# One written order of a fused recurrence and feed-forward kernel exchanged for another

## Chip, cores, metric

One core of a Trainium2 chip. The metric is the device time of one execution in microseconds, taken as the median of several runs; beside it there is one profiled execution, whose trace and page are read here. Its engines are PE (TensorE, with its weight loads shown apart as PEld), DVE (VectorE), ACT (ScalarE), POOL (GpSimd) and SP, which here only issues the transfers.

## What is computed

A gated linear recurrence over 4 sequences of 768 tokens with 8 heads, in chunks, and behind it a feed-forward block on the 3072 tokens of width 256:

```
L = exp(cum[i] - cum[j]) * causal            # cum: running sum of log a
y = (C B^T * L) x + exp(cum) * (C state)     # per chunk and head
state = exp(sum log a) * state + (B * exp(cum_end - cum))^T x
h = y @ w_in                                 # 256 -> 2048
out = softplus(h) @ w_out                    # 2048 -> 256
```

All inputs and the output are float32.

## The kernel before

The 3072 tokens are 24 units of 128 (six to a sequence). A unit needs its decays (on POOL), scores (PE), the product of both (DVE), a state update and the outputs, which are scaled on DVE. The feed-forward part takes the tokens in six blocks j of 512 (four units each) and the hidden width in 16 slices k of 128. Every float32 product of it is made of three matmuls over parts (high x high, high x low, low x high), so the weights, x and the softplus results are split into a high part (an ACT cast) and a low part (a DVE subtraction).

The first 28 projection steps and their surroundings are issued from a text, ORDER. Each word is one step, or one stage of a step that comes again; the digits are its argument:

- la, kb, hc, un, gg, w, gd, cr: transfers issued on SP. w is a piece of the weights (even numbers w_in, odd ones w_out), un a unit's inputs, hc its score operands, gg its growth factors, cr the copies of the split C of a unit into the one buffer c_rows. kb holds constants.
- W: the split of a weight piece, five stages: ACT (two operations), DVE, DVE (the two merges), ACT (high part), DVE (low part, wil or wol). Q: the same for B and C of units from 8 on.
- ft, fr: factors by token and by row (matmuls, then exponentials on ACT; fc is one of their results). D: decays on POOL (the select that writes rm). S: scores. M: scores times decays, in two halves, on DVE (tile m). B, C: scaled B and C (bp, cc). U, T: state and its spread (state, tb). R, I: matmuls of a unit's output. G: the scaling (y on DVE, xh on ACT). X: the low part xl on DVE. gq: growth factors by matmul. zero: c_rows cleared on POOL.
- v, e: for pairs of units from 8 on, the values (update, within) and the ends.
- H: the projection of slice k for the first 256 tokens of block 0. F j.k: the projection (all of it, or its other half where H came before). P j.k: softplus and cast on ACT, low part on DVE. Z j.k: the value step, six matmuls into the two accumulators. K, L: copies of the accumulators of a half block. E: the sums of block 0.
- warmN: N small matmuls on a cleared tile, whose results nothing reads.

Blocks 0 and 1 go through the hidden width in two halves, in the order (0, 0 to 7), (1, 0 to 7), (0, 8 to 15), (1, 8 to 15). Projections, scores, products and updates of the units take their tiles from six PSUM banks, and the two accumulators have one each.

Behind ORDER, from step AHEAD = 28 on, a loop issues one projection and the value step LAG = 4 before it, with the work of units 12 to 23 planned between them. While the flag in_order holds, ACT, DVE and POOL keep the order of the source; from step PINNED on they do not, and the framework's scheduler places their instructions by its own time line. PE and the transfers on SP keep the source's order throughout. In the profile an instruction issued under in_order has line L125 (the helper that pins it), a free one has its own line. A unit from 12 on that is loaded while in_order holds also gets a one-element clearing of its buffer on DVE:

```
if in_order[0] and i >= FIRST:
    V.memset(both[:1, :1, :1], 0)
```

Weight pieces, the operands of later units and one pair of half sums share four buffers (tag wraw); the loads of a piece wait for a free one.

Of the kernel before, what the change touches and what calls it, by code (L numbers as in the profile page):

```python
# [52 lines left out]


ORDER = """
warm8 la w3 w0 hc0 hc1 un2 logr w2 un0 zero loga logr kb un1 growth loga W3 ft0 W3 W0 un3 W3 hc2 S0 W0 ft0 hc3 W0 W3
D0 W0 W3 S1 growth gb gd D1 hc4 M0 W2 un4 gq0 hc5 M0 W0 D2 fr0 gq0 fr2 fr0 ft2 M1 fr2 B1 fr0 B0 I0 W2 fr0 ft2 U0 B2 U1
gq2 U0 B3 C1 U1 G0 S2 gg3 T2 C2 T1 M1 S3 G0 W2 D3 gq2 R1 M2 W2 R2 C3 M2 U2 I1 X0 D4 U2 I2 w1 G1 S4 w4 M3 G1 un6 X1 un5
M3 fr2 hc7 H0 T3 D5 fr2 w6 M4 tl R3 M4 H1 B4 C4 D6 U3 G2 I3 U3 U4 S5 G3 W2 G3 G2 X3 H2 W1 hc6 X2 M5 w5 F0.0 un7 T4 W4
U4 H3 W1 T5 F0.1 C5 B6 W1 R4 P0.0 W4 w7 F0.2 W1 W4 R5 P0.1 W1 F0.3 P0.2 M5 P0.0 U6 I4 W4 U6 D7 I5 P0.1 un9 S6 G5 W6 G4  # L60
gg6 P0.0 S7 W4 P0.3 Z0.0 W6 W5 B7 T7 P0.1 G4 H4 C7 W6 Z0.1 W5 un8 P0.3 M6 P0.2 W5 H5 W6 X4 w8 F0.4 P0.2 R7 P0.3 P0.4
F0.5 W6 Q9 Z0.2 M7 W7 Q9 M7 F0.6 Q9 cr9 M6 G5 D10 gg12 W5 U7 P0.4 I7 U7 D9 Q8 I6 G7 Z0.3 P0.5 X5 G7 P0.6 P0.4 P0.5 W5
F0.7 G6 X7 G6 gg10 Z0.4 X6 Q9 P0.5 w10 F1.0 W7 W7 S9 P1.0 Q8 F1.1 W7 B9 cr8 P0.6 W7 W8 Z0.5 M9 un10 P0.6 P0.7 W8 F1.2
P1.0 P0.7 P1.0 Z0.6 Q8 W8 W10 T8 w9 P0.7 F1.3 Q8 P1.2 W10 P1.2 w12 Z0.7 W8 P1.2 M9 F1.4 L0 W8 D8 P1.1 K0 P1.3 S8 P1.1
F1.5 M8 Q10 P1.1 W12 Z1.0 W10 Q10 w13 P1.4 W12 F1.6 W10 cr10 Q10 W10 W12 Z1.1 W9 M8 un11 C8 D11 W12 F1.7 P1.3 W12 P1.4
Z1.2 P1.7 P1.3 W13 B8 P1.4 F0.8 C9 P1.7 W9 Q11 Q10 Z1.3 P0.8 P1.7 w14 P1.5 v8 P1.5 P1.6 P1.5 W9 F0.9 v8 w15 W13 Z1.4
W13 P0.9 Q11 W9 W13 F0.10 P1.6 P0.8 Z1.5 Q11 P0.8 e8 e8 P0.10 F0.11 W9 P1.6 S10 P0.11 Z1.6 M10 cr11 W14 C10 W13 w11
F0.12 P0.10 B10 W14 P0.9 Q11 Z1.7 W14 S11 K1 F0.13 M11 L1 un13 M10 W11 Z0.8 M11 P0.11 W11 W14 v10 P0.11 W14 P0.13
P0.10 W15 F0.14 v10 C11 P0.13 P0.9 e10 P0.14 F0.15 e10 e10 W11 e10 Z0.9 W15 W11 un12 P0.13 gg8 e10 F1.8 P0.14 W11 W15
Z0.10 W15 P0.12 F1.9 P0.12 P0.15 P0.12 Z0.11 F1.10 P0.15 P0.15 Z0.12 W15 P1.10 P1.10 Z0.13 P1.8 P1.10 e8 P1.9 F1.11  # L70
P0.14 P1.8 e8 Z0.14 e8 P1.11 P1.9 P1.8 P1.9 P1.11 Z0.15 E0 P1.11
"""
HALF = NFT // 2
AHEAD = 28
PINNED = 31
LAG = 4
WRAW = 4
EARLY = 8
# [24 lines left out]
def recurrence_then_ffn(ctx: ExitStack, tc: tile.TileContext, fst, un, alr, w_in, w_out, const, outT):  # L103
# [820 lines left out]
    for s in range(AHEAD, len(steps) + LAG):  # L924
        if s == PINNED:
            in_order[0] = False
# [63 lines left out]
```

## Time and profile before

| | us |
|---|---|
| median of 3 runs | 326.56 |
| lowest, highest | 325.31, 326.64 |
| the profiled execution | 324.59 |
| its span | 322.9 |
| PE busy | 314.8 |
| DVE busy | 201.9 |
| ACT busy | 182.2 |
| POOL busy | 38.6 |

Busy is the time in which an engine executes at least one instruction. Matmuls overlap, so that a busy PE may still start them later than it could; the distance between their starts shows it. The granted clock of PE is in the page and in the answers on stretches of time. A row of the timeline gives the start, the length, the engine, the line, the operation with its tiles, and the number of instructions merged into it; in brackets stands the idle time of the engine before it and what ended it. The 0.98 us before the first matmul and the some 3 us after the last are parts of the span.

### The profile page before, as it was taken

How to read it: one execution, taken by the hardware profiler on the slowest of the kernel's cores; microseconds unless marked ns; L12 is line 12 of the kernel's file. 1: busy time of each engine (PE TensorE's matmuls, PEld its weight loads, DVE VectorE, ACT ScalarE, POOL GpSimd, SP SyncE). 2: the span in 40 equal slices, each digit the busy share in tenths (PEclk: the TensorE clock that was granted, in tenths of full speed). 3: DMA queues.
4: the chain of work that ended last, by engine and by line, in shares of the span. 5: the costliest groups of instructions: out<-in, count | busy, mean ns of one | idle time of the engine just before them, and what ended most of it. 6: DMA issues, size and time to landing. Idle time of an engine off the chain costs nothing.

```text
span 322.9 us, 5266 instructions
## 1 busy us (share of the span) xinstructions
PE 314.8 (98%) x1968; PEld 255.3 (79%) x1968; DVE 201.9 (63%) x354; ACT 182.2 (56%) x333; POOL 38.6 (12%) x42
## 2 busy tenths in 40 slices
PE   7799999999989999999999999999999999999996
PEld 3568878888868888788888788888888888888885
DVE  5999999887793667874646745776653432322222
ACT  5879878895565665555533834745634344544450
POOL 4661030110200001101202101102100000000000
PEclk9999999999999999999999999999999999999999
DMA  7959748553612145344126236135301000100001
GB/s 258 391 175 374 246 130 225 180 167 108 194 52 82 66 149 146 97 143 119 32 100 162 87 110 155 44 106 154 101 0 35 1 2 0 64 1 2 0 0 66
DMA packets 25178, 36.53 MB, mean 113 GB/s; under 512 B 2112, under 2 KB 13504, under 8 KB 25152
## 3 DMA queue, kind: packets, MB, share of 16 engines
q1 hardware_dynamic: 25152, 36.19, 36.4%
q8 instruction: 15, 0.25, 0.3%
q14 instruction: 11, 0.09, 0.1%
HBM read 28.74 MB, written 3.24 MB: 99 GB/s over the span
## 4 chain that ended last, share of the span: by engine, by line
PE 86%; DVE 6%; DMA 4%; ACT 2%; issue 1%; SPq 1%; ACTq 0%; DVEq 0%
PE hp L125 38%; PE acc L125 37%; PE yp L125 6%; PE sp L125 3%; DMA wraw<-in_w_out 3%; DVE w L125 2%; DMA bc<-in_un 1%; PE zp L125 1%; PE end L125 1%; DVE m L125 1%; ACT signs L125 1%; ACT w L125 1%; DVE wol L125 1%; SPq L135 1%; DVE b_rows L288 0%
## 5 line engine op out<-in xcount | busy, mean ns | idle before, releaser
L722 DVE TENSOR_TENSOR gl<-e,gh 128x512 fp32r<-128x512 f32 x65 | 50.9, 787 | 49.0 <-ACT gh L716 48.7
L125 PE MATMUL hp<-xh,wih 128*128 128x512 f32 (+1 forms) x204 | 77.7, 381 | 0.0
L125 PE MATMUL hp<-xh,wil 128*128 128x512 f32 (+1 forms) x204 | 76.9, 377 | 0.6 <-DVE wil L125 0.6
L125 PE MATMUL hp<-xl,wih 128*128 128x512 f32 (+1 forms) x204 | 76.9, 377 | 0.0
L710 ACT ACTIVATE e<-hp 128x512 f32<-128x512 f32 x65 | 38.7, 595 | 64.8 <-PE hp L125 64.2
L125 PE MATMUL acc<-gh,woh 128*128 128x512 f32 x188 | 74.9, 398 | 0.1
L125 PE MATMUL acc<-gl,woh 128*128 128x512 f32 x188 | 73.5, 391 | 0.0
L125 PE MATMUL acc<-gh,wol 128*128 128x512 f32 x188 | 73.2, 390 | 0.0
L125 PEld LDWEIGHTS hp<-xh,wil 128*128 128x128 f32 x204 | 38.3, 188 | 8.2 <-DVE wil L125 1.1
L125 PEld LDWEIGHTS hp<-xh,wih 128*128 128x128 f32 x204 | 38.4, 188 | 7.7 <-DVE y L125 0.8
L125 PEld LDWEIGHTS hp<-xl,wih 128*128 128x128 f32 x204 | 38.4, 188 | 6.8
L716 ACT CAST gh<-e 128x512 fp32r<-128x512 f32 x65 | 40.2, 618 | 5.1 <-PE acc L125 3.5
L125 PEld LDWEIGHTS acc<-gh,woh 128*128 128x128 f32 x188 | 35.4, 188 | 8.5 <-ACT signs L125 0.8
L125 PEld LDWEIGHTS acc<-gh,wol 128*128 128x128 f32 x188 | 35.3, 188 | 7.5
L125 PEld LDWEIGHTS acc<-gl,woh 128*128 128x128 f32 x188 | 35.4, 188 | 6.5 <-DVE gl L722 0.2
L398 POOL TENSOR_SCALAR_AFFINE_SELECT rm<-fc 128x1024 f32<-128x1024 f32 x11 | 16.2, 1477 | 128.2 <-DVE m L453 96.4
L125 DVE TENSOR_TENSOR gl<-e,gh 128x512 fp32r<-128x512 f32 x31 | 21.2, 687 | 10.9 <-ACT gh L125 10.9
L125 POOL TENSOR_SCALAR_AFFINE_SELECT rm<-fc 128x1024 f32<-128x1024 f32 x13 | 18.7, 1443 | 63.7 <-DVE m L125 53.4
L125 ACT ACTIVATE e<-hp 128x512 f32<-128x512 f32 x31 | 18.0, 592 | 12.5 <-PE hp L125 11.0
L125 ACT CAST gh<-e 128x512 fp32r<-128x512 f32 x31 | 18.6, 616 | 5.6 <-PE acc L125 5.4
L125 DVE TENSOR_TENSOR m<-sp,rm 128x512 f32<-128x512 f32 x26 | 17.2, 682 | 1.8 <-PE sp L125 1.2
L453 DVE TENSOR_TENSOR m<-sp,rm 128x512 f32<-128x512 f32 x22 | 14.1, 684 | 3.8 <-PE sp L125 3.8
(104 smaller groups left out, 313.5 us busy)
## 6 DMA issues: line engine op xcount, KB each, us to landing
bc<-in_un SPq DMA_DIRECT2D x16, 512.0 KB
wraw<-in_w_out SPq DMA_DIRECT2D x8, 512.0 KB
wraw<-in_w_in SPq DMA_DIRECT2D x8, 512.0 KB
un<-in_un SPq DMA_DIRECT2D x16, 256.0 KB
out_t<-o SPq DMA_DIRECT2D x9, 256.0 KB
c_rows<-c_all SPq DMA_DIRECT2D x16, 128.0 KB
gg<-gd SPq DMA_DIRECT2D x16, 128.0 KB
c_rows<-kc SPq DMA_DIRECT2D x16, 128.0 KB
```

Of the source, the lines that this page charges most:

```text
L125: return lambda *a, **k: tc.keep_in_program_order(f(*a, **k))
L135: tc.keep_in_program_order(nc.sync.dma_start(out, in_))
L398: Pl.affine_select(out=rm.rearrange("p h c i -> p (h c) i"), in_=fc[:, u].rearrange("p h c -> p (h c)").unsqueeze(2).broadcast_to([P, NH * ...
L453: V.tensor_tensor(mid[i]["m"][:, 4 * g : 4 * g + 4].rearrange("p h t -> p (h t)"), mid[i].pop(("sp", g)), mid[i]["rm"][:, 4 * g : 4 * g + ...
L710: A.activation(e, h, AF.Softplus)
L716: A.copy(gh, e)
L722: V.tensor_tensor(gl, e, gh.bitcast(F32), op=ALU.subtract)
```

## The change

ORDER is replaced by another permutation of the same words, with nine warm-up matmuls in front in place of eight and two single ones between, and PINNED goes from 31 to 37, so that the loop's steps 31 to 36 are issued in source order too.

```
--- before.py
+++ after.py
@@ -53,26 +53,26 @@
 
 
 ORDER = """
-warm8 la w3 w0 hc0 hc1 un2 logr w2 un0 zero loga logr kb un1 growth loga W3 ft0 W3 W0 un3 W3 hc2 S0 W0 ft0 hc3 W0 W3
-D0 W0 W3 S1 growth gb gd D1 hc4 M0 W2 un4 gq0 hc5 M0 W0 D2 fr0 gq0 fr2 fr0 ft2 M1 fr2 B1 fr0 B0 I0 W2 fr0 ft2 U0 B2 U1
-gq2 U0 B3 C1 U1 G0 S2 gg3 T2 C2 T1 M1 S3 G0 W2 D3 gq2 R1 M2 W2 R2 C3 M2 U2 I1 X0 D4 U2 I2 w1 G1 S4 w4 M3 G1 un6 X1 un5
-M3 fr2 hc7 H0 T3 D5 fr2 w6 M4 tl R3 M4 H1 B4 C4 D6 U3 G2 I3 U3 U4 S5 G3 W2 G3 G2 X3 H2 W1 hc6 X2 M5 w5 F0.0 un7 T4 W4
-U4 H3 W1 T5 F0.1 C5 B6 W1 R4 P0.0 W4 w7 F0.2 W1 W4 R5 P0.1 W1 F0.3 P0.2 M5 P0.0 U6 I4 W4 U6 D7 I5 P0.1 un9 S6 G5 W6 G4
-gg6 P0.0 S7 W4 P0.3 Z0.0 W6 W5 B7 T7 P0.1 G4 H4 C7 W6 Z0.1 W5 un8 P0.3 M6 P0.2 W5 H5 W6 X4 w8 F0.4 P0.2 R7 P0.3 P0.4
-F0.5 W6 Q9 Z0.2 M7 W7 Q9 M7 F0.6 Q9 cr9 M6 G5 D10 gg12 W5 U7 P0.4 I7 U7 D9 Q8 I6 G7 Z0.3 P0.5 X5 G7 P0.6 P0.4 P0.5 W5
-F0.7 G6 X7 G6 gg10 Z0.4 X6 Q9 P0.5 w10 F1.0 W7 W7 S9 P1.0 Q8 F1.1 W7 B9 cr8 P0.6 W7 W8 Z0.5 M9 un10 P0.6 P0.7 W8 F1.2
-P1.0 P0.7 P1.0 Z0.6 Q8 W8 W10 T8 w9 P0.7 F1.3 Q8 P1.2 W10 P1.2 w12 Z0.7 W8 P1.2 M9 F1.4 L0 W8 D8 P1.1 K0 P1.3 S8 P1.1
-F1.5 M8 Q10 P1.1 W12 Z1.0 W10 Q10 w13 P1.4 W12 F1.6 W10 cr10 Q10 W10 W12 Z1.1 W9 M8 un11 C8 D11 W12 F1.7 P1.3 W12 P1.4
-Z1.2 P1.7 P1.3 W13 B8 P1.4 F0.8 C9 P1.7 W9 Q11 Q10 Z1.3 P0.8 P1.7 w14 P1.5 v8 P1.5 P1.6 P1.5 W9 F0.9 v8 w15 W13 Z1.4
-W13 P0.9 Q11 W9 W13 F0.10 P1.6 P0.8 Z1.5 Q11 P0.8 e8 e8 P0.10 F0.11 W9 P1.6 S10 P0.11 Z1.6 M10 cr11 W14 C10 W13 w11
-F0.12 P0.10 B10 W14 P0.9 Q11 Z1.7 W14 S11 K1 F0.13 M11 L1 un13 M10 W11 Z0.8 M11 P0.11 W11 W14 v10 P0.11 W14 P0.13
-P0.10 W15 F0.14 v10 C11 P0.13 P0.9 e10 P0.14 F0.15 e10 e10 W11 e10 Z0.9 W15 W11 un12 P0.13 gg8 e10 F1.8 P0.14 W11 W15
-Z0.10 W15 P0.12 F1.9 P0.12 P0.15 P0.12 Z0.11 F1.10 P0.15 P0.15 Z0.12 W15 P1.10 P1.10 Z0.13 P1.8 P1.10 e8 P1.9 F1.11
-P0.14 P1.8 e8 Z0.14 e8 P1.11 P1.9 P1.8 P1.9 P1.11 Z0.15 E0 P1.11
+la warm9 w0 kb hc0 un0 hc2 loga w3 w2 logr loga un1 logr ft0 growth W0 hc1 un2 fr2 ft2 ft0 W0 hc3 W0 D0 S0 fr2 W0 gb
+fr0 W0 S2 D2 growth ft2 M0 gd hc5 fr2 M0 W3 un3 B0 D1 M2 U0 hc4 gq0 fr2 U0 W2 fr0 w4 W3 fr0 B1 gq2 W3 fr0 gq0 U1 W2 S1
+C1 T1 U1 I0 B2 C2 M2 R1 T2 gq2 D3 M1 S3 tl gg3 G0 M1 U2 W3 W2 I1 D4 R2 U2 W2 G1 M3 warm1 G0 I2 G1 X0 S5 C3 T3 G2 X1 S4
+w1 B3 W2 un4 R3 M3 hc6 W4 hc7 warm1 W3 D5 U3 un5 I3 U3 G2 un9 M4 H0 G3 w6 T4 G3 H1 X2 W1 X3 M4 F0.0 W4 D6 H2 P0.0 M5
+C4 F0.1 W4 H3 P0.0 P0.1 W1 F0.2 w5 un6 B4 R4 W1 P0.2 U4 P0.0 W4 I4 U4 W1 S6 M5 un7 P0.2 gg6 W4 D9 P0.1 S7 M6 C5 W1
+F0.3 W6 zero H4 M6 Z0.0 Q9 T5 D7 P0.3 w7 G4 P0.1 R5 F0.4 W6 H5 P0.4 B6 I6 Q9 I5 W6 Q9 U6 Z0.1 G5 C7 w10 Q9 cr9 G5 P0.2
+W6 un8 F0.5 U6 X5 G4 T7 P0.3 Z0.2 M7 P0.4 W6 P0.5 R7 X4 W5 B7 F0.6 M7 P0.4 D8 G6 U7 I7 G6 U7 P0.6 F0.7 G7 W7 P0.3 X6
+W5 Z0.3 G7 P0.6 X7 W7 P0.5 F1.0 W5 Q8 W5 Q8 S9 W5 Q8 F1.1 cr8 M9 W10 W7 w8 Z0.4 P0.6 un11 P0.7 Q8 P0.7 F1.2 W10 W7
+un10 P1.0 P0.7 W7 S8 F1.3 P0.5 W8 W10 B8 Z0.5 w12 P1.2 M8 gg8 P1.1 W8 P1.0 B9 F1.4 W8 Q11 T8 W8 w9 P1.0 Z0.6 W10 M8
+P1.3 M9 D11 P1.3 F1.5 P1.2 P1.3 Q10 D10 Z0.7 C8 P1.5 F1.6 W8 L0 P1.1 Q10 v8 K0 Q10 C9 W12 P1.1 W10 Z1.0 P1.4 Q10 W9
+P1.2 w13 F1.7 cr10 Q11 P1.6 W9 Q11 v8 Z1.1 P1.6 W12 C10 Q11 F0.8 P1.5 w11 P1.5 gg10 Z1.2 W9 W12 w14 P1.6 F0.9 W12 P1.4
+W12 P0.8 B10 Z1.3 P1.4 P1.7 W11 S10 F0.10 P0.9 cr11 W9 P1.7 e8 Z1.4 P1.7 W11 e8 e8 F0.11 W11 gg12 M10 Z1.5 w15 W9 M10
+W14 F0.12 P0.10 W14 S11 P0.10 Z1.6 P0.9 P0.10 W14 F0.13 M11 W14 P0.9 P0.8 P0.11 M11 Z1.7 W11 P0.8 P0.12 v10 K1 C11 L1
+un12 W11 W14 W13 Z0.8 v10 P0.11 e10 e8 F0.14 e10 e10 P0.12 W13 P0.13 Z0.9 P0.12 W15 e10 F0.15 P0.14 e10 P0.14 W13
+Z0.10 P0.14 un13 P0.15 W15 F1.8 W13 P0.11 P0.13 W15 Z0.11 P0.13 P1.8 W15 W13 F1.9 e8 W15 Z0.12 P1.9 P1.8 F1.10 P1.9
+P1.9 Z0.13 P1.8 P0.15 P1.10 P0.15 F1.11 Z0.14 P1.11 P1.11 P1.10 P1.11 Z0.15 E0 P1.10
 """
 HALF = NFT // 2
 AHEAD = 28
-PINNED = 31
+PINNED = 37
 LAG = 4
 WRAW = 4
 EARLY = 8
```

## The prediction

> **What bounds the kernel now.** I read the page's busy lines first, then the stretches, then the matrix unit's waits and the timeline around each of them. Times are us from the span's start; a word of the written order stands for its step (S9, F0.14).
>
> ```profile
> span 322.9 us, 5266 instructions
> PE 314.8 (98%) x1968; PEld 255.3 (79%) x1968; DVE 201.9 (63%) x354; ACT 182.2 (56%) x333; POOL 38.6 (12%) x42
> ```
>
> Next the stretches. The first five lines are of PE alone: stretch, length, PE busy (instructions), granted clock, DMA share, GB/s. The last has all engines: length, PE, weight loads, DVE, ACT, POOL, then clock and DMA.
>
> ```profile
> 0.00:21.20 21.20, 17.19 (x148) 1.00 0.76 267
> 21.20:89.50 68.30, 68.30 (x527) 1.00 0.66 210
> 89.50:92.40 2.90, 2.01 (x10) 1.00 0.03 11
> 109.20:142.00 32.80, 32.67 (x191) 1.00 0.44 136
> 142.00:319.90 177.90, 177.86 (x1024) 1.00 0.22 62
> 20.00:30.00 10.00, 10.00 (x98) 8.11 (x98) 9.72 (x23) 8.11 (x20) 3.42 (x3) 1.00 0.89 320
> ```
>
> TensorE (PE) is the bound: apart from the first 21 us, 0.9 us near 90, 0.13 near 134 and the tail after 319.9 it never stops, at a granted clock of 1.00. Busy time hides part of a wait, since matmuls overlap; below I use the distance between starts. VectorE (DVE) is 9.72 of 10 busy where PE has just begun its projections (20 to 30), so the start-up is a DVE chain. An order can win only in the first 21 us, at the stall near 90 and at the one near 134; all the rest is fixed PE work.
>
> The stall near 90, in the timeline (start, length, engine, operation) with one line of the chain of work (105.29); v10 begins at 87.94, F0.14 follows it:
>
> ```profile
> 80.72 1.29 SPq L135 DMA_DIRECT2D c_rows<-c_all  x2
> 82.06 0.61 SPq L135 DMA_DIRECT2D wraw<-in_w_out  x1
> 86.92 0.66 ACT L125 ACTIVATE w<-wraw 128x512 f32<-128x512 f32 x1 [1.50 <-DMA wraw<-in_w_out]
> 87.80 1.28 POOL L398 TENSOR_SCALAR_AFFINE_SELECT rm<-fc 128x1024 f32<-128x1024 f32 x1
> 88.30 1.32 DVE L125 SCALAR_TENSOR_TENSOR w<-w,signs 128x512 int32<-128x512 int32 x1 [1.26 <-ACT signs L125]
> 90.14 0.68 DVE L125 TENSOR_TENSOR wil<-w,wih 128x512 fp32r<-128x512 f32 x1
> 91.99 0.28 DVE L125 TENSOR_TENSOR cc<-un,fr 128x128 f32<-128x128 f32 x1
> 84.63 0.64 PE L125 MATMUL sp<-c_rows,b_rows 128*128 128x256 f32 x4
> 87.94 0.32 PE L125 MATMUL zp<-un,bp 128*32 128x64 f32 x8
> 89.85 0.40 PE L125 MATMUL hp<-xl,wih 128*128 128x512 f32 x1
> 90.87 0.50 PE L125 MATMUL hp<-xh,wil 128*128 128x512 f32 x1 [0.63 <-DVE wil L125]
> 92.33 0.71 PE L125 MATMUL yp<-cc,tb 128*128 128x128 f32 x4 [0.26 <-DVE cc L125]
> 105.29 1.36 PE hp L125 x6
> ```
>
> Weight piece w11 is issued by SP at 82.06, behind the c_rows copies of unit 11 (80.72). It reaches ACT at 86.92; DVE, in written order, has W11's first merge (88.30) ahead of W14's last step (90.14), so F0.14's third matmul starts 1.02 us after its second where a full pitch is 1.36/6 = 0.23: 0.80 lost. The step behind (92.33) waits for the cc at 91.99, another 0.43. Together 1.23.
>
> **The change, part by part.** The written order has the same steps, but one warm-up matmul more in front and two single ones later, and PINNED goes from 31 to 37. PE's total work is the same apart from those three. So the time is: when F0.0 can start, plus fixed PE work, plus stalls.
>
> *Break-even at F0.0.* These rows carry the start.
>
> ```profile
> 0.98 3.60 PE L125 MATMUL warm<-some 128*32 128x512 bf16 x8 [0.98 <-POOL some L125]
> 4.50 1.86 PE L125 MATMUL fp<-both_logs,kc 128*128 128x96 f32 x10
> 8.03 0.85 ACT L125 ACTIVATE fc<-fp 128x384 f32<-128x384 f32 x1
> 8.95 3.48 POOL L125 TENSOR_SCALAR_AFFINE_SELECT rm<-fc 128x1024 f32<-128x1024 f32 x2 [3.50 <-ACT ft L125]
> 6.76 0.69 DVE L125 SCALAR_TENSOR_TENSOR w<-w,signs 128x512 int32<-128x512 int32 x1 [1.21 <-ACT signs L125]
> 9.53 1.76 DVE L125 TENSOR_TENSOR wol<-w,woh 128x512 fp32r<-128x512 f32 x1
> 11.21 1.28 DVE L125 TENSOR_TENSOR m<-sp,rm 128x512 f32<-128x512 f32 x2
> 15.28 0.21 DVE L125 COPY state<-zp 128x64 f32<-128x64 f32 x1
> 25.24 0.75 DVE L125 TENSOR_TENSOR xl<-y,xh 128x256 fp32r<-128x256 f32 x2
> 24.02 0.29 PE L125 MATMUL zp<-un,bp 128*32 128x64 f32 x8
> 25.30 0.39 PE L125 MATMUL hp<-xh,wih 128*128 128x256 f32 x1
> 26.12 0.28 PE L125 MATMUL hp<-xh,wih 128*128 128x256 f32 x1
> wraw<-in_w_in SPq DMA_DIRECT2D x8, 512.0 KB
> kb<-in_const SPq DMA_DIRECT2D x1, 102.5 KB
> ```
>
> F0.0 starts now at 26.12, behind the second remainder X (25.24 and its 0.75, done at 25.99). The new order has two steps fewer ahead of it: U4 (24.02 to 24.24, 0.2) and H2 (25.30 to 26.12, 0.72 without the gap). They follow later, so break-even for F0.0 is 26.12 - 0.92 = 25.2.
>
> *The new start.* ACT now splits only W0 before it turns to fc, where it did W3 and W0 (the first piece landed for DVE's 6.76; w0 takes its place). ft0's matmuls wait for nine warm-ups: 4.50 + 0.43 = 4.93, plus about 1.7, so fc can start at 6.75 instead of 8.03. POOL's first select starts 0.92 after fc as now (8.95 against 8.03): 7.67, and at half of 3.48 each, rm0 is there at 9.4. S0 is done by then: its load hc0 stays the fourth, but with kb's 102.5 KB ahead of it in place of a weight piece's 512. DVE has W0's last step in between, so I put the first M0 at 9.9, against 11.21 now. From there to the last X before F0.0 the new order gives DVE 15 operations of 512 columns, 12 of 256 and 9 small ones. By start-to-start distances (1.28 for two is 0.60 and a last 0.68; 0.75 for two is 0.33 and 0.42; 0.2 small) that is 9.0 + 4.0 + 1.8 = 14.8. The same count over the present stretch, 14 + 11 + 11, gives 8.4 + 3.6 + 2.2 = 14.2, and it took 25.99 - 11.21 = 14.8; so 4% are waits. 14.8 x 1.04 = 15.4, and the last X ends at 25.3. F0.0 at 25.3 against 25.2: +0.1. From both sides: M0 at 9.4 with no waits gives 24.2 (-1.0); W0's last step stretched like the 1.76 at 9.53 puts M0 at 10.6 and F0.0 at 26.0 (+0.8).
>
> *The warm-ups.* 3.60/8 = 0.43 each here. The ninth delays ft0 by 0.43, which stands in the start above. The two single ones lie before I2 and before U3, where PE waits for DVE's M and G steps: 0, and 0.86 if that cover is gone.
>
> *The later banks.* S5 and S4 come earlier and hold four of six PSUM banks; H1 then needs M4's first half, H2 needs G3, both ahead of X3 on DVE. Nothing beyond X3's time.
>
> *The stall near 90.* In the new order w11 stands before w14 and both before unit 11's c_rows copies; SP reaches w14 once W12's second merge frees its buffer, eight DVE operations (about 4) behind v8; between v8 and F0.14 PE has 16 steps of 1.36, 21.8. So w14 has some 17, where w11 took 86.92 - 82.06 = 4.9. W11's merges are on DVE before M10, W14's last step directly behind K1. K1 waits for Z1.7; after Z1.7 PE still has v10 (1.6, from 87.94 to F0.14's start at 89.53), Z0.8 (1.36) and e10's matmuls (0.4) before F0.14, and DVE has K1, C11, W11's and W14's last steps, 0.7 + 0.3 + 0.6 + 0.6 = 2.2 after it. So F0.14 does not wait: -1.2 (bounds -1.23 and 0). What is late next: e10 needs v10's state and tb on DVE, queued behind those 2.2 and 0.5 itself, while PE has 2.9: +0.1.
>
> *S8 after S9.* There is one c_rows buffer. The new order puts S8 only F1.1, Z0.4 and F1.2 behind S9: 3 x 1.36 = 4.1. Unit 11's copies were issued at 80.72 and used by S11 at 84.63 without a wait, so 3.9 suffice: 0 (bounds 0 and the 1.5 by which a queue of one weight load would delay it).
>
> *Other queues.* c_rows' zeroing moves on POOL behind seven selects; its first use is the copies of unit 9, some 5 us later: 0. On SP the early loads are reordered to first need (w0, kb, hc0, un0, hc2 before w3); gg3 and w1 keep their places; hc6 waits for S5 and S4 to free its buffer and holds up un5, un9, w6 and w5, of which the first is wanted over 10 us of PE work later: 0.
>
> *PINNED 37.* Six more steps are issued in source order on DVE, ACT and POOL, and two more loads (units 15, 16) get a 0.06 us marker on DVE. What it touches in the trace is the end of token block 1:
>
> ```profile
> 132.43 1.43 DVE L288 SCALAR_TENSOR_TENSOR b_rows<-bc,kb,b_rows 128x512 fp32r<-128x512 f32 x1
> 133.78 0.68 DVE L793 TENSOR_TENSOR o<-acc,half 128x512 f32<-128x512 f32 x1
> 134.00 0.39 PE L125 MATMUL acc<-gh,wol 128*128 128x512 f32 x1
> 134.51 0.50 PE L125 MATMUL acc<-gh,woh 128*128 128x512 f32 x1
> ```
>
> DVE put a b_rows of 1.43 ahead of the second sum, so PE started 0.51 after its last matmul instead of 0.23: 0.28 lost. In source order both sums stand directly behind the last value step, with two projections (2.7) as cover. Free instructions of later steps may still slip in, so I take -0.2 (bounds -0.28 and +0.3; the values of a step follow four steps behind, which hides a late DVE).
>
> Sum: +0.1 - 1.2 + 0.1 - 0.2 = -1.2. Profiled span 322.9 becomes 321.7. That run took 324.59, of which 1.7 lies outside the span and is not touched; it stands 2.0 below the median 326.56 of the timed runs. Against the median: 325.4.
>
> [...] The 1.76 at 9.53 and the 1.32 at 88.30 (0.69 is usual) both read two SBUF tiles while POOL had a select (8.95, 87.80); the m at 11.21, whose sp is in PSUM, kept its usual pace under the second select. [...]
>
> **The rivals.**
>
> 1. *The stall moves rather than goes.* S8 waits for unit 8's copies, or F0.14 for w14, by about 1.2: time as before, 326.6. For it: SP is one queue and the present stall came from just such a place. Against: the margins above.
>
> 2. *Slower: DVE is held by POOL throughout the start.* Five selects (units 2, 1, 3, 4, 5) run between M0 and X3. If each held one operation by 0.63 (1.32 - 0.69), F0.0 would come at 9.9 + 14.8 + 3.2 = 27.9, 2.7 behind break-even: -1.3 + 2.7 = +1.4, 328.0. It decides from F0.0 at 26.5, where it has eaten the 1.3. Against: the present stretch lost 0.6 with as many selects.
>
> 3. *The start leads too.* M0 at 9.4 and few waits: F0.0 at 24.2, sum -2.3, 324.3. For it: W3's last step, stretched now, no longer stands before M0.
>
> **How the numbers follow.** The forecast has 0.45 (its own range -2.0 to -0.4), rival 1 0.16, rival 2 0.16, rival 3 0.23. 0.5% is 1.6 us, about what this measurement can tell from no change. Faster by more: rival 3 and a third of the forecast, 0.38. Slower by more: rival 2 nearly half, and the worse end of rival 1, plus late loads that I do not see, 0.17. Else 0.45. Range: rival 3 with its run-to-run 0.8 below, 323.5, to rival 2, 327.9.
>
> **What would show it.** Right: rm0 starts near 7.7, F0.0 near 25.3; PE's waits list no wil near 90; PE busy without gap from F0.0; the two sums ahead of b_rows near 133. Wrong: F0.0 after 26.5; a wait of sp for c_rows at S8; a DMA wait on ACT before W11 or W14; new gaps between 109 and 142, where the source order now rules.

## The result: slower by 1.4%, and the profile after

The changed kernel took 330.51 us in the median of four runs (329.28 to 330.73), the kernel before 325.94 beside it on the same chip: ratio 1.0136, interval 1.0093 to 1.018. 325.4 was forecast. The ratios here and below leave out the few executions that fell into a slower state, one of them (455.37) among the six of e9. Times below are us from the span's start, as before.

The page of the changed kernel, its busy lines, PE's row of slices and the granted clock, then TensorE's (PE's) waits (engine, tile, what it waited for: total, times, longest):

```profile
span 328.7 us, 5269 instructions
...
PE 318.4 (97%) x1971; PEld 256.8 (78%) x1971; DVE 201.1 (61%) x356; ACT 181.9 (55%) x333; POOL 41.0 (12%) x42
...
PE   8999999999999999499999999999999999999996
...
PEclk9999999999999999989999999999999999999999
...
PE acc L125 <- DVE o L125: 4.6, 1, 4.6
PE warm L125 <- POOL some L125: 1.0, 1, 1.0
PE sums L125 <- DMA kb<-in_const: 0.6, 1, 0.6
PE hp L125 <- ACT e L125: 0.5, 1, 0.5
PE yp L125 <- DVE tb L125: 0.3, 1, 0.3
```

The span is 5.8 longer, and one slice shows it: the seventeenth, where PE is 4 tenths busy, with a clock of 8 tenths in a slice behind it. The stretches around it (length, PE busy, granted clock, DMA share, GB/s):

```profile
24.50:109.12 84.62, 83.72 (x566) 1.00 0.52 165
109.12:133.21 24.09, 24.09 (x110) 1.00 0.41 120
133.21:144.04 10.83, 6.22 (x62) 0.84 0.31 84
144.04:325.70 181.66, 181.66 (x1043) 1.00 0.22 64
```

Up to step F1.12 (109.12, against 109.24 before) and behind 144.04 (181.66, against 181.73) the two kernels are alike. All of the loss lies between: 10.83 us with 6.22 busy. PE's own rows there:

```profile
133.21 0.39 PE L125 MATMUL hp<-xh,wil 128*128 128x512 f32 x1
138.21 0.65 PE L125 MATMUL acc<-gh,woh 128*128 128x512 f32 x1 [4.61 <-DVE o L125]
138.66 0.63 PE L125 MATMUL acc<-gl,woh 128*128 128x512 f32 x1
139.09 0.63 PE L125 MATMUL acc<-gh,wol 128*128 128x512 f32 x1
...
142.87 0.40 PE L125 MATMUL acc<-gl,woh 128*128 128x512 f32 x1
```

The first value step of block 2 waits until the sums of block 1 have freed the accumulators. From start to start that is 5.00 where a matmul's pitch is 0.23: 4.77 lost. Then the matmuls come every 0.43 instead of every 0.23 until about 142.5. Why the sums (o) are late stands in the timelines of ScalarE (ACT) and VectorE (DVE), the second with GpSimd's (POOL) one row of that time:

```profile
126.34 0.60 ACT L125 ACTIVATE e<-hp 128x512 f32<-128x512 f32 x1 [1.47 <-PE hp L125]
129.75 0.72 ACT L286 ACTIVATE c_all<-bc,kb 128x512 fp32r<-128x512 f32 x1 [2.82 <-DMA bc<-in_un]
130.38 0.60 ACT L125 CAST gh<-e 128x512 fp32r<-128x512 f32 x1
```

```profile
130.51 0.75 DVE L288 SCALAR_TENSOR_TENSOR c_all<-bc,kb,c_all 128x512 fp32r<-128x512 f32 x1 [4.91 <-ACT c_all L286]
131.18 0.69 DVE L125 TENSOR_TENSOR gl<-e,gh 128x512 fp32r<-128x512 f32 x1
132.18 0.69 DVE L125 TENSOR_TENSOR gl<-e,gh 128x512 fp32r<-128x512 f32 x1 [0.31 <-ACT gh L125]
132.79 1.28 DVE L125 TENSOR_TENSOR m<-sp,rm 128x512 f32<-128x512 f32 x2
133.99 0.28 DVE L125 TENSOR_TENSOR bp<-un,ft 128x128 f32<-128x128 f32 x1
134.18 0.28 DVE L125 TENSOR_TENSOR cc<-un,fr 128x128 f32<-128x128 f32 x1
134.39 1.35 DVE L413 TENSOR_TENSOR bp<-un,ft 128x128 f32<-128x128 f32 x1
135.66 0.48 DVE L429 TENSOR_TENSOR cc<-un,fr 128x128 f32<-128x128 f32 x2
136.06 0.74 DVE L125 SCALAR_TENSOR_TENSOR kc<-bc,kb,kc 128x512 fp32r<-128x512 f32 x1
136.73 0.74 DVE L125 SCALAR_TENSOR_TENSOR b_rows<-bc,kb,b_rows 128x512 fp32r<-128x512 f32 x1
137.39 1.28 DVE L125 TENSOR_TENSOR o<-acc,half 128x512 f32<-128x512 f32 x2
...
134.20 1.41 POOL L398 TENSOR_SCALAR_AFFINE_SELECT rm<-fc 128x1024 f32<-128x1024 f32 x1 [12.13 <-DVE m L125]
```

Two things stand in front of the sums:

- A. The free split of unit 15 (L286, L288) has been put ahead of the ordered cast gh of a block 2 product. It needs the load bc, which lands at 129.7, and ACT idles 2.82 for it with the cast behind it; DVE idles 4.91.
- B. In the source unit 13's products with its scaled B and C (132.79 to 134.39) and the split of unit 14 (kc, b_rows; 136.06 to 137.39) are issued at step 34, the sums at step 35. With the marker at 37 all of them, 2.9 of DVE time, go ahead of the sums. Between the two the scheduler has put free scaled B and C of later units (L413, L429; 134.39 to 136.06, 1.7), whose place in the source is step 38 or later: the same kind of overtaking as in A. Before, the free scheduler did unit 14's split in DVE's idle time around 124, and the sums stood at 131.83 and 133.78.

### The profile page after: what moved, and what is told of

Read it like the earlier page. It is cut to its first block, busy times and chain, and to the rows that moved or that the text cites. A ratio compares the mean times of both kernels' runs of the same rounds, so it can differ in the third digit from the quotient of the medians.

```text
span 328.7 us, 5269 instructions
## 1 busy us (share of the span) xinstructions
PE 318.4 (97%) x1971; PEld 256.8 (78%) x1971; DVE 201.1 (61%) x356; ACT 181.9 (55%) x333; POOL 41.0 (12%) x42
## 3 DMA queue, kind: packets, MB, share of 16 engines
HBM read 28.74 MB, written 3.24 MB: 97 GB/s over the span
## 4 chain that ended last, share of the span: by engine, by line
PE 73%; DVE 11%; DMA 7%; ACT 3%; issue 3%; SPq 2%; DVEq 0%; ACTq 0%
PE acc L125 33%; PE hp L125 32%; PE yp L125 5%; DMA wraw<-in_w_in 3%; DVE m L125 2%; DMA wraw<-in_w_out 2%; PE sp L125 2%; SPq L135 2%; DVE w L125 2%; DMA bc<-in_un 1%; ACT signs L125 1%; ACT gh L125 1%; DVE y L125 1%; PE end L125 1%; PE zp L125 1%
## 5 line engine op out<-in xcount | busy, mean ns | idle before, releaser
L398 POOL TENSOR_SCALAR_AFFINE_SELECT rm<-fc 128x1024 f32<-128x1024 f32 x10 | 15.9, 1589 | 133.4 <-DVE m L453 89.3
L125 POOL TENSOR_SCALAR_AFFINE_SELECT rm<-fc 128x1024 f32<-128x1024 f32 x14 | 21.4, 1539 | 61.9 <-DVE m L125 58.9
L125 DVE TENSOR_TENSOR m<-sp,rm 128x512 f32<-128x512 f32 x28 | 18.7, 680 | 0.0
L125 ACT ACTIVATE w<-wraw 128x512 f32<-128x512 f32 x16 | 10.7, 671 | 10.6 <-DVE wol L125 5.6
```

The costliest lines, as they stand in the source:

```text
L125: return lambda *a, **k: tc.keep_in_program_order(f(*a, **k))
L398: Pl.affine_select(out=rm.rearrange("p h c i -> p (h c) i"), in_=fc[:, u].rearrange("p h c -> p (h c)").unsqueeze(2).broadcast_to([P, NH * ...
```

## Experiments

The theory is A and B together, and for the slow matmuls, that they follow from the wait itself (C). Rivals: that the new ORDER costs it, that one of A and B is all of it, that a late transfer sets the time wherever the sums stand, or that the slow pace has a cause of its own.

**e1: the new order with the old marker.**

```
-PINNED = 37
+PINNED = 31
```

> The new ORDER with PINNED back at 31. Theory (the longer source order made the loss): the 4.8 us wait of the value step at 133 for the block's sums goes, and with it the halved matmul pace behind it (about 1.3 us); the span falls from 328.7 to about 322.7, the ratio to the kernel before is 0.997 to 1.002. Rival (the new ORDER's later loads delay unit 15's operands, whatever is pinned): a wait of 3 us or more for the sums stays, ratio 1.008 or more.

324.51 (ten runs, 324.02 to 325.93) against 326.57: ratio 0.9945, interval 0.9917 to 0.9974. The wait near 134 is one small row among the others:

```profile
134.57 0.50 PE L125 MATMUL acc<-gh,woh 128*128 128x512 f32 x1 [0.23 <-DVE o L793]
```

So the order is not what loses; it wins about 0.55%, and this kernel is faster than both.

**e2: the old order with the new marker.** In the kernel before:

```
-PINNED = 31
+PINNED = 37
```

> The old ORDER with PINNED at 37 alone. Theory: the wait for the sums near 133 appears here too, 4 to 5 us, with halved matmul pace behind it; span 322.9 + 5.5 = 328.4, ratio 1.014 to 1.02. The stall near 90 stays as before. Rival (ORDER is to blame, or both are needed): no wait over 1 us near 133, ratio within 0.997 to 1.004.

332.19 (four runs), ratio 1.0166, interval 1.0113 to 1.0218. The same wait for o is there, 4.1 us over the pitch, with ACT idle 2.15 for unit 15's bc in the same place, and slow matmuls behind it. The marker alone does the damage, in either order. The profiled span (330.4) is 2.0 above the one expected: this execution's start was 2.2 later than that of the profile before, behind a wait of 3.9 for the first head tile. That belongs to the old order, as e11 shows.

**e3: unit 15's split in the source's order (A taken away).** In split_whole of the changed kernel:

```
+was, in_order[0] = in_order[0], in_order[0] or i == 15
 ...
+in_order[0] = was
```

> As the changed kernel (PINNED 37), but the split of unit 15 keeps its place in the source too, so that its first ACT operation cannot slip in front of the casts of block 2. Theory A (that one free operation waits for its transfer at the head of ACT's queue, and the pinned casts, products and sums stand behind it): ACT never waits for the transfer of bc near 127, DVE's idle time of 4.9 us goes, and the sums are done near 131 to 133; wait at 133 at most 0.5 us, span about 322.7, ratio 0.996 to 1.003. Theory B (the source order itself puts the products of unit 13 and the split of unit 14, 2.9 us of DVE work, in front of the sums): a wait of 1 to 3 us stays, ratio 1.004 to 1.01.

327.88 (ten runs, 326.19 to 329.49), ratio 1.0028, interval 0.9994 to 1.0063. The profiled execution is the slowest of the ten. ACT's cast, DVE's sums and PE:

```profile
129.11 0.62 ACT L125 CAST gh<-e 128x512 fp32r<-128x512 f32 x1
...
134.97 1.27 DVE L125 TENSOR_TENSOR o<-acc,half 128x512 f32<-128x512 f32 x2
...
132.63 0.39 PE L125 MATMUL hp<-xh,wil 128*128 128x512 f32 x1
135.80 0.76 PE L125 MATMUL acc<-gh,woh 128*128 128x512 f32 x1 [2.78 <-DVE o L125]
136.36 0.63 PE L125 MATMUL acc<-gl,woh 128*128 128x512 f32 x1
```

The wait for bc is gone, and the lost time falls from 4.77 to 2.94 (135.80 - 132.63 - 0.23). So A is worth 1.8 of the wait. The 2.9 left is what still stands ahead of o: the ordered products and split of B (2.9 of DVE time) and the free scaled B and C between them (131.97 to 133.65, 1.7); their shares in the wait are not told apart here. The ratio lies a little below the 1.004 to 1.01 expected. Half of the ten runs kept a granted clock of 1.000 (326.19 to 327.82); the other half, with the profiled one, had 0.990 to 0.995 (327.93 to 329.49).

**e4: the marker at 35,** so that the sums are free and the steps up to 34 ordered.

```
-PINNED = 37
+PINNED = 35
```

> The new ORDER with PINNED 35: the split of unit 15 is free and again first on ACT before the cast of step 32, but the sums are free too and stand on DVE right behind it, ahead of unit 13's products. Theory A: ACT and DVE still wait for the transfer until about 130, but the sums follow at 130 to 132.5, so that the wait at 133 is at most 1 us: span 322.5 to 324, ratio 0.996 to 1.004. Theory B as well gives a small wait. If the transfer itself came later (the marker on DVE for unit 15 delays its issue from 125.2 to 125.9), ACT's wait is as long as in the changed kernel, 2.8 us.

325.45 (ten runs), ratio 0.9967, interval 0.9939 to 0.9994. The first sum now runs at 129.76, ahead of the products, and the second at 132.77, behind them but ahead of the split, and no wait for o is among PE's listed waits, the smallest of which is 0.3. ACT still idles 1.54 for bc. A late bc therefore costs little as long as the sums do not stand behind what it holds up.

**e5: A and B taken away, marker at 37.** e3's edit, and around finish(j) of the values step:

```
+was, in_order[0] = in_order[0], in_order[0] and j != 1
 finish(j)
+in_order[0] = was
```

> The changed kernel with two lifts of the order: unit 15's split keeps the source's order (as in the third experiment) and the two sums of block 1 alone are issued as free instructions, so that the planner may put them ahead of unit 13's products and unit 14's split. Theory (two parts: the free split of unit 15 that overtakes the casts, about 1.8 us of the wait; the source's own order, which puts unit 13's products, its scaled B and C and unit 14's split in front of the sums, about 2.9 us): both parts are gone, the wait of TensorE for o falls from 4.77 to at most 0.3 us, no slow matmuls follow, and the time is 324 to 325 us, ratio 0.992 to 0.998, like the new order with the marker at 31. Rival (the wait comes from the late arrival of bc15 or from the tightness of the new written-out order, not from the sums' place): a wait of 2 us or more stays and the ratio is 1.00 or above.

324.71 (twelve runs, 324.15 to 325.35), ratio 0.9951, interval 0.9932 to 0.997. The time is e1's; the wait was expected at 0.3 or less and came out at 0.76. The two sums and PE:

```profile
129.75 0.69 DVE L795 TENSOR_TENSOR o<-acc,half 128x512 f32<-128x512 f32 x1 [1.91 <-PE acc L125]
...
133.83 0.68 DVE L795 TENSOR_TENSOR o<-acc,half 128x512 f32<-128x512 f32 x1
...
133.41 0.39 PE L125 MATMUL acc<-gh,wol 128*128 128x512 f32 x1
134.56 0.50 PE L125 MATMUL acc<-gh,woh 128*128 128x512 f32 x1 [0.76 <-DVE o L795]
134.90 0.40 PE L125 MATMUL acc<-gl,woh 128*128 128x512 f32 x1
```

The first sum stands ahead of the products, as soon as PE is done with its accumulator; the second still has one bp of 1.35 in front. The kernel before has a wait of this size too in its later profiles (0.9 in e11, 0.8 in e12). All the other instructions of steps 31 to 36 are in source order here and cost nothing measurable.

**e6: only the sums free;** unit 15's split stays where it overtakes.

> The changed kernel with the two sums alone issued as free instructions; unit 15's free split still stands ahead of the pinned casts of block 2. The two-part theory: the casts and so the products of block 2 are as late as in the changed kernel, but the sums do not stand behind them; the planner decides how early they go. If the sums stand ahead of unit 13's products the wait for o is at most 1 us and the ratio 0.993 to 1.000. If the late casts by themselves hold the sums' step (the values need gh and gl of block 2 too, free at 131.2 in the changed kernel against 133.2 when they are wanted), a wait of at most 0.5 us for gl is seen in place of it. Rival (the split of unit 15 ahead of the casts is the whole cause): the wait stays at 3 us or more, ratio 1.005 or above.

324.6 (twelve runs), ratio 0.9956, interval 0.9935 to 0.9976; a wait of 0.71. The rival that A is all of it fails: with A in place, but the sums out of the queue, the loss is gone. The 4.77 is the sum of what stands ahead of two instructions, not a price of any of them.

**e7: e3 with unit 14's split two steps earlier.** Unit 13's scores then read unit 14's C, since both use the one buffer c_rows, and so are not the ones asked for; the work is the same in kind and number.

```
-        plan(max(s - 4, AHEAD), split_whole, i)
+        plan(32 if i == 14 else max(s - 4, AHEAD), split_whole, i)
```

> The third experiment's kernel (split of unit 15 in the source's order) with unit 14's split two steps earlier in the source, at step 32 in place of 34. In the third experiment its two VectorE instructions (0.67 and 0.66 us) and the wait for ScalarE's gh stood ahead of the sums. The two-part theory: they go into VectorE's idle time before the products, and scaled B of unit 14 goes behind the first sum, so the wait of 2.94 us falls by 1.3 to 2.7 us, to 0.2 to 1.6, with no slow matmuls if it falls under about 1 us; ratio 0.994 to 1.000. Rival (the sums' place behind the products counts and not what fills VectorE before them): the wait stays above 2.5 us and the ratio at about 1.003.

325.09 (twelve runs), ratio 0.9981, interval 0.9956 to 1.0006. There is no wait for o; the sums stand at 133.00 and 134.68. A new one of 0.85 has come at 130.34, where scores wait for the copies into c_rows. From the start of the products to the first sum DVE takes 1.59 in place of e3's 4.60: the split (1.3) is gone from there, and the free scaled B and C (1.7) now run between the two sums. So the queue ahead of the sums is what cost, as B says; that PE itself came later, by the new wait, helped to hide the rest.

**e8: the wait filled.** In the changed kernel 18 matmuls of the wide shape, whose results nothing reads, ahead of step 36's value matmuls (in the loop, before values(s)):

```
+        if s == PINNED - 1:
+            fill(18)   # PE.matmul(w, wih[:, 0, :P], xh[:, 0, :512]) each
```

> The changed kernel with 18 further matmuls (128x512, about 0.23 us each, 4.1 us in all) that nothing reads, on TensorE where it waits for the sums. They take the place of the wait's idle time and leave its end to VectorE. If the slow matmuls after the wait (0.43 us each for about 4 us) come from the idle time itself, they are gone: the wait left is about 0.7 us, the matmuls behind it run at 0.23 us at once, and the span falls by 1.3 to 1.8 us to about 327, ratio 1.002 to 1.009. Rival (the slow matmuls come from what runs beside them then, or the clock falls for a reason of its own): they stay at 0.4 us, the span is 328.5 or more and the ratio 1.012 to 1.018.

327.97 (twelve runs), ratio 1.0051, interval 1.003 to 1.0072: with 4.1 us more of PE work the kernel is nearer to the one before than without (1.0136). No wait for o is left, and the value matmuls run at 0.23 at once.

**e10: half the filler** (fill(9)).

> The changed kernel with 9 instead of 18 matmuls that nothing reads, ahead of the wait for the sums: 2.1 us of the wait filled, about 2 us left idle at its end. If the slow matmuls follow from the length of the unbroken idle time, and 2 us is short enough, they are gone and the time equals that with 18 matmuls (ratio 1.003 to 1.007). If 2 us is already too long (the third experiment had slow matmuls behind a wait of 2.8 us, the fourth and fifth none behind one of 0.8 to 1.0), some 1 to 1.6 us of it stay, and the ratio is 1.008 to 1.014.

327.38 (twelve runs), ratio 1.0021, interval 0.9995 to 1.0046. PE waits 1.6 at the end of the filler and then runs at full pace:

```profile
132.74 2.20 PE L125 MATMUL fill<-xh,wih 128*128 128x512 f32 x9
136.40 0.50 PE L125 MATMUL acc<-gh,woh 128*128 128x512 f32 x1 [1.46 <-DVE o L125]
136.74 0.40 PE L125 MATMUL acc<-gl,woh 128*128 128x512 f32 x1
```

So the slow pace behind this wait follows from its idle time (C): with 4.61 idle the value matmuls came every 0.43, with 1.46 (e10) or none (e8) every 0.23. Its size: from the first value matmul of block 2 to the last matmul's end the changed kernel takes 187.5 (138.21 to 325.7), e8 185.9 (137.09 to 323.0, its span of 326.0 less the 3.0 behind the last matmul in the changed kernel). That is 1.6. In all twelve runs of either filler kernel the granted clock was 0.998 or more, in the changed kernel's four 0.990 to 0.995. In the filler kernels the sums also came earlier than in the changed kernel's profile: in e8 by 1.1 (136.31), behind a bc that was as much earlier (c_all at 129.44 against 130.51), and in e10 the first value matmul, which waits for them, came 1.8 earlier (136.40 against 138.21); whether the filler does that or the run is not shown.

**e9: what the new order wins.** e1 gained 2.06 us by the medians, while its profiled span (322.9) equals that of the profiled execution before. The guess was the first head tile's load, which PE waits for only in the old order. In the kernel before:

```
-warm8 la w3 w0 hc0 hc1 un2 ...
+warm8 la hc0 w3 w0 hc1 un2 ...
```

> The kernel before (old order, marker at 31) with one word of its order moved: the first unit's head tile is loaded ahead of the first two weight loads instead of behind them. In the profile of the kernel before, TensorE waits 1.3 us for that tile; in the second experiment, which has the same old order, it waits 3.9 us, and the whole start is 2.2 us later. Theory (what the new order wins over the kernel before, 0.55% with the marker at 31, is this load, whose landing differs from run to run): the wait is under 0.5 us, the runs spread less and the time falls to 324.5 to 325.5 us, ratio 0.993 to 0.998. Rival (the win comes from the stall near 90 us and the rest of the order): the ratio stays within 0.002 of 1.

331.48 (six runs; 330.9 without the one left out), ratio 1.0131, interval 1.0081 to 1.0181. This fits neither the guess nor its rival: it is slower. The wait moved to the next head tile:

```profile
10.30 1.13 PE L125 MATMUL sp<-head_in_l 64*128 64x512 f32 x4 [3.24 <-DMA head_in_l<-in_fst]
```

The first weight piece reached ACT at 8.11 instead of 5.41, with the factors (fc) queued behind its split there. The early loads share the transfer time (a DMA share of 1.04 from 5 to 13 in the profile of before); here one put first made others late. Behind these waits PE's granted clock was lower: 7 tenths in the page's slice from 8.3 to 16.5 and 5 tenths in the next, to 24.8. Ten matmuls fp took 2.43 there (16.36), where the profile of before has 1.33 (12.59), so slow matmuls in the start are part of the loss. The word alone settles nothing on the new order.

**e11, e12: the kernel before, profiled again.**

> The kernel before, unchanged, for a second profile of it (its profiled execution took 324.59 us, 2.0 below the median of its runs). If its start differs from run to run, as the other kernel with the old order suggests (3.9 us of waiting for the first head tile in place of 1.3), a profile of an execution near the median of 326.5 shows a wait for head_in_l of 2 to 4 us and matmuls at about 0.84 us in place of 0.42 behind it. If the difference lies elsewhere, the wait stays near 1.3 us and another stage is longer by about 2 us.

> The kernel before, unchanged, a third profile, for the same question: the length of the wait for the first head tile goes with the time of the execution, or it does not.

One run each, 327.11 and 325.37. The scores of the first unit in the first profile of before, in e11 and in e12:

```profile
7.69 1.99 PE L125 MATMUL sp<-head_in_l 64*128 64x512 f32 x8 [1.32 <-DMA head_in_l<-in_fst]
```

```profile
8.84 3.78 PE L125 MATMUL sp<-head_in_l 64*128 64x512 f32 x8 [3.14 <-DMA head_in_l<-in_fst]
```

```profile
8.00 3.59 PE L125 MATMUL sp<-head_in_l 64*128 64x512 f32 x8 [2.14 <-DMA head_in_l<-in_fst]
```

Waits of 1.3, 2.1 and 3.1 go with spans of 322.9, 323.7 and 325.4; behind the two longer ones the scores take 3.6 to 3.8 instead of 2.0 (a score matmul 1.06 in the median instead of 0.59), and the granted clock over the first 10 us and the next 10 is 0.89 and 0.94 (e12) and 0.85 and 0.81 (e11), where the first profile has 1.00 in both. The execution profiled first was a lucky one. The timed runs bear this out. Of 75 runs of the kernel before beside these experiments, the 7 with a granted clock of 0.998 or more have a median of 325.2, the 31 at 0.993 to 0.995 one of 326.0, the 32 at 0.988 to 0.990 one of 326.8, and the 5 below one of 329.1; of e1's ten runs nine have 1.000. So some 1.4 of e1's 2.06 (326.57 against 325.2) go with the lower clock. The new order loads this tile behind 102 KB of constants instead of a second weight piece, and none of its profiles shows a wait for it. That this wait, with the slow matmuls behind it, is most of what the new order wins is the likeliest reading; it is not shown by an experiment, and moving that load alone (e9) did not bring it.

## Why the prediction was wrong

*PINNED 37, taken at -0.2 with bounds of -0.28 and +0.3: the step that failed.* It measured +6.0 within the profile: the wait went from 0.28 to 4.77 (+4.5), and the slow pace added some 1.5. Less the 0.1 of the order up to F1.12, that is about the 5.8 by which PE's last matmul ends later (319.86 and 325.7). The prediction looked at what the source puts between the last value step and the sums, and found nothing; it did not list what the source puts ahead of them on the same queue. Step 34's products and unit 14's split (B) were in the source to be read; with the free scaled B and C between them they made 2.9 of the wait by e3. It said that the value steps' lag hides a late DVE; the accumulators are not covered by that lag, since the first value step of block 2 needs the sums that follow the last of block 1. "Free instructions of later steps may still slip in" named A, but at most 0.3 was allowed for it; the split that slipped in brought its own wait for a transfer (1.8 by e3). And the price of a wait was taken as its length, without the slow matmuls behind it. The sign list did name this place: "new gaps between 109 and 142, where the source order now rules."

*The order, worked out at -1.0 (+0.1 - 1.2 + 0.1), measured -0.1 in the profile at F1.12.* Rows of the changed kernel for its terms:

```profile
7.53 3.50 POOL L125 TENSOR_SCALAR_AFFINE_SELECT rm<-fc 128x1024 f32<-128x1024 f32 x2 [3.02 <-ACT ft L125]
...
8.90 0.99 DVE L125 TENSOR_TENSOR wil<-w,wih 128x512 fp32r<-128x512 f32 x1 [0.56 <-ACT wih L125]
9.81 1.27 DVE L125 TENSOR_TENSOR m<-sp,rm 128x512 f32<-128x512 f32 x2
...
24.50 0.28 PE L125 MATMUL hp<-xh,wih 128*128 128x256 f32 x1
...
56.49 0.50 PE L125 MATMUL hp<-xh,wih 128*128 128x512 f32 x1 [0.45 <-ACT e L125]
...
90.85 0.71 PE L125 MATMUL yp<-cc,tb 128*128 128x128 f32 x4 [0.33 <-DVE tb L125]
```

- The start went by its steps: the select at 7.53 (7.67 worked out; 4.93 and 1.7 make 6.63, where fc did start, and not the 6.75 that was used), the first M0 at 9.81 (9.9), F0.0 at 24.50 (25.3, within 24.2 to 26.0, nearer to the third rival's). Its second matmul came 0.28 late, so the start gave -0.4 against the break-even of 25.2, where +0.1 was worked out.
- The stall near 90 went as described: no wait for wil, and what is late next is e10, which waits for tb. The size was off: 0.50 is left where +0.1 was allowed, so the term is -0.7 and not -1.1.
- A wait that was costed at nothing came up: at 56.49 a projection waits for a PSUM bank that softplus still reads, 0.6. Another 0.4 is spread over small steps and is not traced.
- S8 behind S9, the warm-ups and c_rows' zeroing cost nothing, as said.

*The base.* 1.2 was taken off the median of 326.56 although the terms came from an execution 2.0 below it. The profile of before did not show the longer load wait of its usual run, and so neither what the new order would save there. By the medians the order is worth -2.06 (e1), about the third rival's -2.3, and the whole change +4.6 in place of the profiles' +5.8.

*DVE beside the selects.* The wil of 8.90 took 0.99 against 0.69 under the select of 7.53, and the bp of 134.39 took 1.35 under the select of 134.20, against 0.28 just before it; e3 and e5 have the same bp of 1.35 (131.97 and 132.55) under selects of 131.78 and 132.37. The bp cost about 1 us of the queue ahead of the sums. But a select beside it does not settle which instruction is held. In the changed kernel a merge of W at 25.37 ran on beside the select of 25.58 and took its usual 0.68, and the merge at 26.57, beside the same select, took 1.15. In e4 the same bp took 0.29, and the two cc that came later took 0.96 instead of 0.48; e6 shows the same. What makes them longer is not shown by these runs.

```profile
132.56 0.29 DVE L413 TENSOR_TENSOR bp<-un,ft 128x128 f32<-128x128 f32 x1
...
133.37 0.96 DVE L429 TENSOR_TENSOR cc<-un,fr 128x128 f32<-128x128 f32 x2
```

*The rivals.* None of the three had the loss. The slower one put it into the start.

## What to carry over

Where an order is pinned, list for each instruction that frees a buffer the bound engine needs (here two sums) everything ahead of it on its in-order engine, from earlier steps too, with the transfers that each waits for; a boundary between ordered and free instructions also lets free ones with unlanded inputs overtake ordered ones (here unit 15's split, for whose bc ACT idled 2.82). Then look at pinning all but those few instructions: two sums set free took the ratio from 1.0136 to 0.9956 here (e6). And take a second profile before building on the first when its execution lies well off the median.

## What the runs showed of the chip

Behind a pause of TensorE the matmuls could come more slowly for a time, so that the pause cost more than its length. Behind the 4.61 of the changed kernel those of 512 columns came every 0.43 instead of every 0.23; the granted clock was 0.86 from 138.2 to 138.4, 0.50 from 138.4 to 141.7 and 1.00 from 141.8. Read over longer stretches, it was 0.91 from 126 to 146 in the changed kernel and in e2; in the starts, over the first 10 us and the next 10, it was 0.89 and 0.94 in e12, 0.85 and 0.81 in e11, 0.88 and 0.78 in e2, and 1.00 in both in the first profile of before.

The length of the pause alone does not settle it. Behind 1.46 (e10) and 0.76 (e5) the value matmuls, after a first step of 0.34, went on every 0.23. Behind 2.14 (e12) eight score matmuls took 3.59 instead of 1.99, and behind 2.78 (e3) value matmuls came every 0.43. But in e2 three matmuls came 0.23 to 0.30 apart behind a pause of 3.94 before the pace fell, and in e9 four kept the full pace behind one of 3.24 (1.13 for the four, as at 5.93), while the eight gp behind the next pause there, of 2.52, took 2.07, where the profile of before has 1.16. What decides when the clock falls is not shown by these runs.
